# One fused kernel, one list of steps per slot: scaled keys, state and the low part of g ahead in the list, and the sums of squares one slot later

## The chip, the cores and the metric

The kernel runs on 1 core of one Trainium2 chip. A core has a matrix engine (PE, with its weight loads shown apart as PEld), a vector engine (DVE), an activation engine (ACT), a general engine (POOL) and a queue engine that issues DMAs (SP). Each runs its own list of instructions in order and waits at an instruction until what it needs is there. The metric is device time in microseconds (us) of one execution.

## The reference

Three stages follow each other: a gated linear attention, a feed-forward block with a cosine, and a gated feed-forward block on normalised rows.

```python
f = 1 / (1 + exp(-f_logit))                      # q, k, v, f_logit: (4, 8, 768, 48)
for t in range(768):
    state = f[t][:, None] * state + outer(k[t], v[t])
    y[t] = q[t] @ state                          # x = heads side by side: (3072, 384)
h = x @ w_in                                     # w_in (384, 2048)
x = (h * cos(h)) @ w_out                         # w_out (2048, 384)
rms = sqrt(mean(x * x, axis=-1) + 1e-6)
xn = x / rms * rms_g
g = xn @ w_gate                                  # w_gate, w_val (384, 1536)
out = (silu(g) * (xn @ w_val)) @ w_out2          # out (3072, 384)
```

## The kernel before

Every large product is made of three products of rounded parts: high times high, low times high and high times low. So each operand is split: ACT casts the high part, and POOL (or DVE) subtracts it to get the low part.

**Slots.** The first feed-forward block walks over 6 blocks of 512 rows and, in each, over 16 groups of 128 hidden columns. One group is a slot; slots 0 to 95 are these. Slots 96 to 167 are those of the second feed-forward block (6 blocks of 12). A slot n of the first kind does, by engine: 9 matmuls for h on PE (`m1_h`, L603, key `H`); on ACT the whole turns of the cosine's argument (`kint`, L612, `k`); on DVE the rest of the division (`wrap`, L618, `w`); on ACT the cosine (L624, `s`); on DVE g (L629, `g`); in the next slot the high part gh on ACT (L637, `hi`) and the low part gl on POOL (L644, `lo`); and two slots later 9 matmuls with `w_out` on PE (`m1_out`, L654). The h of a slot goes to one of two PSUM banks, so `H` of slot n+2 waits for g of slot n; gh and gl have two buffers each.

**Attention in between.** The attention runs in steps of 128 rows (24 steps; steps 0 to 4 are mostly done ahead, in a prologue). From slot 0 to slot 79 each slot takes one of the four pieces of a step on PE (key `P`, `piece_pe`): piece 0 turns the scaled keys (L348), piece 1 makes the scores (L357), piece 2 has nothing left to do in steps 9 and later, piece 3 makes the outputs and the next state's sum. Slot n has piece (n+1) mod 4. What the other engines do for a piece stands in the slot after it: ACT copies the turned keys out of PSUM (`kn`, L424), makes the gates (`tanh` in block 0: L267, L269; `grd` later: L255, L267); DVE runs two scans (`scan`: L281 makes E, L290) and scales k and q (`kt` L303, `qt` L312), adds the state (`st`, L455, L459); POOL copies each step's end of E (`pall`, L286, part of `scan`), spreads v (`vtl`, L292) and scales the state (`Tz`, L329, part of `cy`). All PSUM banks of the attention come from a ring of three, so a bank must be emptied before its third successor is taken.

**Weights.** In block 0 two weight tiles are decoded per slot, in the last block one (keys `t`, `x`, `f`): ACT L547, DVE L559 and L563, ACT L577, POOL L578.

**Sums of squares.** After a block, `m1_evac` (key `act`) empties three accumulators (L664 on DVE, L666 on ACT), POOL squares and adds (L674, L677; key `po`), and PE sums over partitions with a matmul of ones (`m1_sum`, L682, key `pe`), into the next bank of the ring. ACT copies the row (L684), and DMAs and POOL (L699, L700) make the reciprocal roots. `finish` sets in which slot each of these stands.

**The order.** Nothing schedules this: the strings of `SLOT` (block 0, blocks 1 to 4, block 5) and `SLOT2` (first block and the others of the second part) are the order in which a slot's keys are issued, and each engine gets its instructions in that order.

Of the kernel before, what the change touches and what calls it, by code (L numbers as in the profile page):

```python
# [27 lines left out]


SLOT = (  # L30
# [3 lines left out]
)  # L34
SLOT2 = (
    "gv pe t f dv x f sg t u act uh ul po x out ev",
    "gv pe ok act sg dv u uh ul po out ev",
)
PROLOGUE = (
# [10 lines left out]
def kernel(  # L50
# [15 lines left out]
    B, H, S, D = q.shape  # L66
# [52 lines left out]
    xh = [pp.tile([128, KD, 512], F32R, name=f"xh{i}") for i in range(2)]  # L119
    xl = [pp.tile([128, KD, 512], F32R, name=f"xl{i}") for i in range(2)]  # L120
# [8 lines left out]
    am = [ap_.tile([128, 512], F32, name=f"am{i}") for i in range(2)]  # L129
# [38 lines left out]
    st = {}  # L168
# [500 lines left out]
    def m1_store(j, x2):  # L669
        t0, N = blocks[j]  # L670
        nc.sync.dma_start(out=x2_d[:, t0:t0 + N].rearrange("(c p) t -> p c t", p=128), in_=x2)
# [15 lines left out]
    def m1_put(j, r):  # L687
        t0, N = blocks[j]
        nc.sync.dma_start(out=ss_d[t0:t0 + N].unsqueeze(0), in_=r)
# [7 lines left out]
    def m1_rinv(j, c):  # L697
        t0, N = blocks[j]
        nc.gpsimd.tensor_scalar(c, c, 1.0 / DM, EPS, op0=ALU.mult, op1=ALU.add)  # L699
        nc.gpsimd.tensor_tensor(out=c, in0=c, in1=mh.to_broadcast([128, N // 128]), op=ALU.pow)  # L700

    def m1_root(j, c):
        t0, N = blocks[j]
        nc.sync.dma_start(out=ri_d[t0:t0 + N].rearrange("(c p) -> p c", p=128), in_=c)
# [7 lines left out]
    gv = {}  # L712
# [122 lines left out]
    if True:  # L835
# [74 lines left out]
        pe_at, act_at, post_at, dve_at = {}, {}, {}, {}  # L910

        def at(table, slot, fn, *a):
            table.setdefault(slot, []).append((fn, a))
# [7 lines left out]
        held = {}  # L921
# [5 lines left out]
        def set_(key, fn, *a):  # L927
            held[key] = fn(*a)
# [5 lines left out]
        for n, (w, u) in enumerate(units):  # L934
            s = first + n * (4 * N2) // len(units)
# [3 lines left out]
        def finish(j, s, short):  # L939
            at(act_at, s + (1 if short else 2), lambda: set_((j, "x2"), m1_evac, j))  # L940
            at(post_at, s + 2, lambda: m1_store(j, held[j, "x2"]))
            for n, (fn, m) in enumerate(
                ((m1_sq, 0), (m1_sq, 1), (m1_add, 1), (m1_sq, 2), (m1_add, 2))
            ):
                at(post_at, s + 3 + n, lambda fn=fn, m=m: fn(held[j, "x2"], m))
            at(pe_at, s + 8, lambda: set_((j, "r"), m1_sum, j, held.pop((j, "x2"))))
            at(post_at, s + 9, lambda: m1_put(j, held.pop((j, "r"))))
            at(post_at, s + 10, lambda: set_((j, "c"), m1_get, j))
            at(post_at, s + 11, lambda: m1_rinv(j, held[j, "c"]))
            at(post_at, s + 12, lambda: m1_root(j, held.pop((j, "c"))))  # L950

        def norm(jj, s):
            at(post_at, s, m2_load, jj)
# [7 lines left out]
        for j, (t0, N) in enumerate(blocks):  # L961
# [21 lines left out]
            for i in range(N1):  # L983
# [42 lines left out]
                if len(outs) > 2:  # L1026
                    m1_out(*outs.pop(0))
                slot += 1
            finish(j, slot, final)
        m1_hi(*gp)  # L1030
        m1_lo(*gp)
# [283 lines left out]
```

## Time and profile before

| | |
|---|---|
| runs | 1029.33, 1031.47, 1030.81 us; median 1030.81 |
| profiled execution | 1034.35 us, span 1032.6 us |
| PE busy | 987.7 us (96%) |
| DVE busy | 631.2 us (61%) |
| ACT busy | 424.9 us (41%) |
| POOL busy | 327.8 us (32%) |

The profiled execution has 1.75 us around its span. The shares of busy time are means over stages that differ: up to about 568 us the first feed-forward block runs with the attention in between, and after that the second one alone. A busy PE includes matmuls that overlap, and matmuls at the lower of the two clock levels.

### The profile page before, as it was taken

To read this page: it belongs to the slowest core of one execution; us is meant where nothing else is said; L and a number is where in the kernel's file an instruction comes from. 1 tells how busy PE (TensorE), PEld (TensorE's weight loads), DVE (VectorE), ACT (ScalarE), POOL (GpSimd) and SP (SyncE) were. 2 spreads that over 40 slices of the span, in tenths; PEclk is the share of its full clock that TensorE was granted. 3 is DMA by queue.
4 is the path that set the end of the run, shared out by engine and by line. 5 is a ranking of instruction groups with operands and counts; after the bars stand their busy time and mean duration, and the time that the engine had idled before them with its cause. 6 is when DMAs were issued, how large, how long until landed. Compare 5 with 4: busy or idle time off the path is not lost.

```text
span 1032.6 us, 16330 instructions
## 1 busy us (share of the span) xinstructions
PE 987.7 (96%) x6286; PEld 819.1 (79%) x6286; DVE 631.2 (61%) x955; ACT 424.9 (41%) x747; POOL 327.8 (32%) x374
## 2 busy tenths in 40 slices
PE   7788999999899999989999999999999999999997
PEld 6666777778777777768877788888888888888886
DVE  6898976777777877775478666335335335335222
ACT  4466664445454454544667544212212212222111
POOL 2466654543533533363478354001001001001000
PEclk9899999999999999999999999999999999999999
DMA  8885323223222323311333453343343343332000
GB/s 163 195 198 135 85 52 81 51 53 100 65 64 51 86 61 72 95 23 17 108 117 92 138 169 87 92 133 92 108 133 94 114 139 92 123 117 62 31 1 34
DMA packets 123857, 96.14 MB, mean 93 GB/s; under 512 B 69238, under 2 KB 103030, under 8 KB 123772
## 3 DMA queue, kind: packets, MB, share of 16 engines
q1 hardware_dynamic: 123772, 95.03, 34.2%
q8 instruction: 51, 0.84, 0.3%
q14 instruction: 34, 0.28, 0.1%
HBM read 85.54 MB, written 9.46 MB: 92 GB/s over the span
## 4 chain that ended last, share of the span: by engine, by line
PE 67%; DVE 13%; ACT 7%; issue 4%; DMA 3%; POOL 3%; SPq 2%; DVEq 0%; ACTq 0%; POOLq 0%
PE bank L757 29%; PE bank L793 15%; PE bank L654 10%; PE bank L603 8%; DVE wrap L618 2%; DVE g L629 2%; ACT wrap L624 1%; DMA v_sb<-in_v_dram 1%; DVE E L281 1%; ACT gh L637 1%; ACT kint L612 1%; DVE ft L290 1%; POOL gl L644 1%; DVE qt L312 1%; PE bank L401 1%
## 5 line engine op out<-in xcount | busy, mean ns | idle before, releaser
L654 PE MATMUL bank<-gh,wo 128*128 128x512 f32 x576 | 208.3, 416 | 0.0
L771 DVE SCALAR_TENSOR_TENSOR u<-bank,sg 128x512 f32<-128x512 f32 x72 | 49.7, 691 | 201.3 <-PE bank L757 201.3
L644 POOL TENSOR_TENSOR gl<-g,gh 128x512 fp32r<-128x512 f32 x96 | 126.6, 1319 | 68.1 <-ACT gh L637 66.3
L654 PEld LDWEIGHTS bank<-gh,wo 128*128 128x128 f32 x576 | 111.2, 193 | 27.8 <-issue 1.6
L654 PE MATMUL bank<-gl,wo 128*128 128x512 f32 x288 | 117.9, 409 | 10.3 <-POOL gl L644 10.1
L757 PE MATMUL bank<-xh,wo 128*128 128x512 f32 x360 | 122.8, 395 | 0.0
L766 ACT ACTIVATE sg<-bank 128x512 f32<-128x512 f32 x72 | 43.1, 599 | 172.6 <-PE bank L757 172.6
L741 POOL TENSOR_TENSOR xl<-x2b,xh 128x512 fp32r<-128x512 f32 x18 | 24.2, 1344 | 283.1 <-ACT xh L740 283.1
L624 ACT ACTIVATE wrap<-wrap,cb 128x512 f32<-128x512 f32 x96 | 69.3, 722 | 101.1 <-DVE wrap L618 98.6
L778 ACT CAST uh<-u 128x512 fp32r<-128x512 f32 x72 | 44.7, 622 | 152.2 <-DVE u L771 152.0
L637 ACT CAST gh<-g 128x512 fp32r<-128x512 f32 x96 | 59.5, 620 | 100.3 <-DVE g L629 82.4
L629 DVE SCALAR_TENSOR_TENSOR g<-bank,wrap 128x512 f32<-128x512 f32 x96 | 66.0, 688 | 43.4 <-ACT wrap L624 40.5
L618 DVE SCALAR_TENSOR_TENSOR wrap<-bank,kint 128x512 f32<-128x512 f32 x96 | 65.8, 686 | 37.2 <-ACT kint L612 36.6
L784 DVE TENSOR_TENSOR ul<-u,uh 128x512 fp32r<-128x512 f32 x72 | 50.8, 705 | 48.9 <-ACT uh L778 48.9
L757 PEld LDWEIGHTS bank<-xh,wo 128*128 128x128 f32 x360 | 67.6, 188 | 14.6
L654 PEld LDWEIGHTS bank<-gl,wo 128*128 128x128 f32 x288 | 55.6, 193 | 28.5 <-POOL gl L644 16.4
L612 ACT ACTIVATE kint<-bank,cb 128x512 int32<-128x512 f32 x96 | 65.9, 686 | 27.7 <-PE bank L603 27.1
L793 PE MATMUL bank<-wo,uh 128*128 128x384 f32 x288 | 74.1, 338 | 0.0
L757 PE MATMUL bank<-xl,wo 128*128 128x512 f32 x180 | 71.0, 394 | 0.0
L793 PEld LDWEIGHTS bank<-wo,uh 128*128 128x128 f32 x288 | 52.7, 188 | 3.5 <-issue 0.5
L487 DVE SCALAR_TENSOR_TENSOR wacc<-stage,wacc 128x384 int32<-128x384 int32 x68 | 50.9, 748 | 0.7
L578 POOL TENSOR_TENSOR wo<-wx,wo 128x384 fp32r<-128x384 f32 x32 | 34.0, 1063 | 52.3 <-ACT wo L577 51.0
(343 smaller groups left out, 2222.3 us busy)
## 6 DMA issues: line engine op xcount, KB each, us to landing
stage<-in_moe_w_out_dram SPq DMA_DIRECT2D x56, 384.0 KB, 3.4
stage<-in_moe_w_gate_dram SPq DMA_DIRECT2D x24, 384.0 KB, 3.2
stage<-in_moe_w_val_dram SPq DMA_DIRECT2D x24, 384.0 KB, 3.2
stage<-in_moe_w_in_dram SPq DMA_DIRECT2D x16, 384.0 KB, 3.3
nat<-in_f_logit_dram SPq DMA_DIRECT2D x48, 96.0 KB, 3.0
nat<-in_k_dram SPq DMA_DIRECT2D x48, 96.0 KB, 2.3
nat<-in_q_dram SPq DMA_DIRECT2D x48, 96.0 KB, 2.2
v_sb<-in_v_dram SPq DMA_DIRECT2D x24, 192.0 KB, 2.7
```

Source lines behind the costliest of these rows:

```text
L487: nc.vector.scalar_tensor_tensor(out=wacc, in0=hi, scalar=1 << 30, in1=wacc, op0=ALU.bitwise_xor, op1=ALU.bitwise_and,)
L603: nc.tensor.matmul(t, l[:, 128 * kk:128 * (kk + 1)], r[:, kk, 0:N], start=idx == 0, stop=idx == 3 * KD - 1,)
L612: nc.scalar.activation(out=kt, in_=hb[j, i], func=AF.Identity, scale=INV2PI * UNIT, bias=cb[:, 0:1])
L618: nc.vector.scalar_tensor_tensor(out=w, in0=hb[j, i], scalar=INV2PI * UNIT, in1=kt, op0=ALU.mult, op1=ALU.subtract)
L624: nc.scalar.activation(out=w, in_=w, func=AF.Sin, scale=2.0 * math.pi, bias=cb[:, 1:2])
L629: nc.vector.scalar_tensor_tensor(out=g, in0=hb.pop((j, i)), scalar=UNIT, in1=w, op0=ALU.mult, op1=ALU.mult)
L637: nc.scalar.copy(out=h, in_=g)
L644: nc.gpsimd.tensor_tensor(out=l, in0=g, in1=h.bitcast(F32), op=ALU.subtract)
L654: nc.tensor.matmul(acc[m][:, 0:N], lw[:, cs], r, start=i == 0 and x == 0, stop=i == N1 - 1 and x == 2,)
L757: nc.tensor.matmul(t[y], l[:, 128 * kk:128 * (kk + 1)], r[:, kk, :], start=idx == 0, stop=idx == 3 * KD - 1,)
L784: nc.vector.tensor_tensor(out=l, in0=u, in1=h.bitcast(F32), op=ALU.subtract)
L793: nc.tensor.matmul(o2[tt][:, 0:DM], lu[:, cs], r, start=i == 0 and x == 0, stop=i == N2 - 1 and x == 2,)
```

## The change

Only the order changes. In block 0's list (`SLOT[0]`) the keys `st kn` come ahead of `tanh`, and `lo` comes right behind `hi`. In the list of blocks 1 to 4 `kn` comes first, and `lo` right behind `hi`. In the first list of the second part `act` comes first. `finish` puts the matmul of the sums, and the four steps behind it, one slot later.

```diff
 SLOT = (
-    "xh xl tanh hi H t kn x kt qt cy am st scan P k f w x grd f s t lo g po",
-    "tanh hi act H kn ff st kt xh xl qt cy am P k w grd scan s lo dv g pe po",
+    "xh xl st kn tanh hi lo H t x kt qt cy am scan P k f w x grd f s t g po",
+    "kn tanh hi lo act H st xh xl ff kt qt cy am P k w grd scan s dv g pe po",
     "act H hi k w lo P dv t pe s x g f po",
 )
 SLOT2 = (
-    "gv pe t f dv x f sg t u act uh ul po x out ev",
+    "act gv pe t f dv x f sg t u uh ul po x out ev",
     "gv pe ok act sg dv u uh ul po out ev",
 )
...
-            at(pe_at, s + 8, lambda: set_((j, "r"), m1_sum, j, held.pop((j, "x2"))))
-            at(post_at, s + 9, lambda: m1_put(j, held.pop((j, "r"))))
-            at(post_at, s + 10, lambda: set_((j, "c"), m1_get, j))
-            at(post_at, s + 11, lambda: m1_rinv(j, held[j, "c"]))
-            at(post_at, s + 12, lambda: m1_root(j, held.pop((j, "c"))))
+            at(pe_at, s + 9, lambda: set_((j, "r"), m1_sum, j, held.pop((j, "x2"))))
+            at(post_at, s + 10, lambda: m1_put(j, held.pop((j, "r"))))
+            at(post_at, s + 11, lambda: set_((j, "c"), m1_get, j))
+            at(post_at, s + 12, lambda: m1_rinv(j, held[j, "c"]))
+            at(post_at, s + 13, lambda: m1_root(j, held.pop((j, "c"))))
```

The first place is ACT in slot 12 (block 0), one of the slots with a piece 1. `kn` is the copy of the turned keys, the two `ft` rows are `tanh`, `gh` is the high part, and `wi15h` a weight's high part.

```order
 L624 ACTIVATE wrap<-wrap,cb 128x512
 L577 CAST wo<-wx 128x384
+L424 COPY kn<-bank_80 128x512
 L267 ACTIVATE ft_129<-bank_81 128x4x128
 L269 ACTIVATE ft_129<-ft_129,cb 128x4x128
 L637 CAST gh<-g 128x512
 L577 CAST wi15h<-wx 128x384
-L424 COPY kn<-bank_80 128x512
 L547 ACTIVATE wx<-stage,cb 128x384
 L612 ACTIVATE kint<-bank_77,cb 128x512
```

The copy moves ahead of four instructions, and `tanh` now stands behind it.

The second place is ACT from slot 24 to slot 26 (block 1): `kn` again, and `ssr`, the copy of the row of sums that the matmul of the sums made.

```order
 L624 ACTIVATE wrap<-wrap,cb 128x512
-L637 CAST gh<-g 128x512
 L424 COPY kn<-bank_80 128x512
+L637 CAST gh<-g 128x512
 L612 ACTIVATE kint<-bank_77,cb 128x512
 L255 ACTIVATE E,low<-ft_130,cb 128x4x128
 L267 ACTIVATE ft_130<-ft_130 128x4x128
 L624 ACTIVATE wrap<-wrap,cb 128x512
+L637 CAST gh<-g 128x512
+L612 ACTIVATE kint<-bank_78,cb 128x512
+L624 ACTIVATE wrap<-wrap,cb 128x512
 L684 COPY ssr<-bank_80 1x512
```

`kn` no longer waits behind the high part, and `ssr` stands one slot's work later, as its matmul does on PE.

The third place is POOL from slot 35 to slot 37 (block 2), first before, then now. `gl` is the low part, `Tz` the scaled state, `x2` the squares and their sums, `pall` the end of E.

```order
L329 TENSOR_TENSOR Tz_136<-Sn_2737,pall_87 48x4x32 x2
L329 TENSOR_TENSOR Tz_136<-Sn_2737,pall_87 48x4x16 x2
L644 TENSOR_TENSOR gl_2766<-g_2714,gh_2726 128x512
L674 TENSOR_TENSOR x2_2655<-x2_2655 128x512
L286 COPY pall_87<-E_2810 128x4
L644 TENSOR_TENSOR gl_2819<-g_2768,gh_2780 128x512
L674 TENSOR_TENSOR x2_2655<-x2_2655 128x512
```

```order
L644 TENSOR_TENSOR gl_2728<-g_2714,gh_2726 128x512
L329 TENSOR_TENSOR Tz_136<-Sn_2739,pall_87 48x4x32 x2
L329 TENSOR_TENSOR Tz_136<-Sn_2739,pall_87 48x4x16 x2
L674 TENSOR_TENSOR x2_2657<-x2_2657 128x512
L644 TENSOR_TENSOR gl_2784<-g_2768,gh_2782 128x512
L286 COPY pall_87<-E_2812 128x4
L674 TENSOR_TENSOR x2_2657<-x2_2657 128x512
```

Each low part moves ahead of the slot's other work on POOL: ahead of `Tz` in one slot, and ahead of `pall`, which waits for DVE's first scan, in the next.

## Rows read from the trace of the kernel before

**Rows 1.** Busy time in two stretches: start:end, length, PE, PEld, DVE, ACT, POOL, PEclk.

```profile
48.86:142.00 93.14, 81.39 (x588) 63.53 (x592) 85.05 (x130) 63.32 (x120) 61.03 (x60) 0.93 0.51 129
177.08:462.59 285.51, 273.59 (x2229) 216.44 (x2228) 223.21 (x326) 135.06 (x232) 122.79 (x149) 0.99 0.27 65
```

**Rows 2.** The same view, slots 24, 32, 40, 56, 72, 88; 33, 37; 97, 98.

```profile
192.19:202.00 9.81, 7.91 (x37) 5.79 (x36) 7.32 (x13) 4.82 (x9) 2.50 (x3) 0.83 0.41 95
237.25:242.70 5.45, 5.45 (x35) 4.27 (x34) 3.38 (x5) 4.08 (x8) 0.00 (x0) 1.00 0.59 141
279.78:287.68 7.90, 6.34 (x37) 4.65 (x36) 5.47 (x9) 4.83 (x9) 1.16 (x1) 1.00 0.48 115
366.95:374.03 7.08, 6.34 (x37) 4.65 (x36) 4.66 (x8) 4.83 (x9) 0.00 (x0) 1.00 0.54 130
453.08:462.59 9.51, 7.97 (x37) 5.55 (x36) 7.03 (x13) 4.82 (x9) 2.21 (x3) 0.82 0.01 2
530.45:537.79 7.34, 5.28 (x21) 3.68 (x20) 5.92 (x6) 4.26 (x9) 5.17 (x5) 1.00 0.19 54
242.70:246.89 4.19, 4.19 (x19) 3.30 (x18) 4.09 (x8) 1.67 (x3) 2.99 (x4) 1.00 0.00 0
262.64:268.85 6.21, 4.44 (x19) 3.30 (x18) 5.40 (x10) 3.21 (x7) 3.43 (x5) 1.00 0.23 59
576.19:584.25 8.06, 6.52 (x31) 5.35 (x30) 5.25 (x9) 3.62 (x7) 2.02 (x2) 1.00 0.35 104
584.25:590.54 6.29, 6.29 (x31) 5.48 (x31) 2.91 (x6) 2.10 (x5) 1.02 (x1) 1.00 0.68 226
```

**Rows 3.** PE's waits from 177 to 463 us: for whom, in total, times, longest.

```profile
PE bank L682 <- ACT kn L424: 5.7, 4, 1.9
PE bank L654 <- POOL gl L644: 5.1, 6, 1.8
```

**Rows 4.** The one wait of this kind in the whole trace.

```profile
PE bank L682 <- POOL x L677: 2.1, 1, 2.1
```

**Rows 5.** Timeline of slot 36 and its end: start, length, engine, [idle before <-releaser].

```profile
260.57 0.62 ACT L637 CAST gh<-g 128x512 fp32r<-128x512 f32 x1 [0.88 <-PE bank L357]
261.09 0.58 ACT L424 COPY kn<-bank 128x512 f32<-128x512 f32 x1
261.57 0.69 ACT L612 ACTIVATE kint<-bank,cb 128x512 int32<-128x512 f32 x1
...
262.30 0.69 DVE L618 SCALAR_TENSOR_TENSOR wrap<-bank,kint 128x512 f32<-128x512 f32 x1 [0.79 <-ACT kint L612]
...
265.69 0.68 DVE L629 SCALAR_TENSOR_TENSOR g<-bank,wrap 128x512 f32<-128x512 f32 x1
...
265.42 0.19 POOL L286 COPY pall<-E 128x4 f32<-128x4 f32 x1 [7.30 <-DVE E L281]
265.57 1.26 POOL L644 TENSOR_TENSOR gl<-g,gh 128x512 fp32r<-128x512 f32 x1
```

**Rows 6.** Timeline of slot 12 (block 0), the same columns.

```profile
126.09 0.72 ACT L269 ACTIVATE ft<-ft,cb 128x512 f32<-128x512 f32 x1
127.64 0.57 ACT L424 COPY kn<-bank 128x512 f32<-128x512 f32 x1
...
126.84 2.17 DVE L281 TENSOR_TENSOR_SCAN E<-ft,seed 128x516 f32<-128x516 f32 x1 [0.78 <-ACT ft L269]
...
128.27 1.16 PE L357 MATMUL bank<-qt,kt 48*128 48x128 f32 x14 [2.02 <-ACT kn L424]
```

**Rows 7.** DVE's two scans from 177 to 463 us: busy us, mean ns | idle.

```profile
L290 DVE TENSOR_TENSOR_SCAN ft<-ft,seed 128x516 f32<-128x516 f32 x13 | 19.6, 1505 | 0.0
L281 DVE TENSOR_TENSOR_SCAN E<-ft,seed 128x516 f32<-128x516 f32 x14 | 17.3, 1233 | 0.5
```

**Rows 8.** Timeline of slot 97, DVE and PE.

```profile
581.24 1.28 DVE L664 TENSOR_SCALAR x<-bank 128x512 f32<-128x512 f32 x2
...
582.07 0.58 PE L793 MATMUL bank<-xunit,uh 128*128 128x384 f32 x2 [1.54 <-ACT uh L778]
```

## The prediction

> **What bounds the kernel now.** I read the busy time by stretch first. In both stretches of [rows 1] PE looks nearly full, but who is full beside it differs. From 48.86 to 142 us (block 0, slots 0 to 14) DVE is busy for 85.05 of 93.14 us, PE for 81.39; DVE also holds the decode there. From 177.08 to 462.59 us (slots 21 to 72, most of blocks 1 to 4) PE is busy for 273.59 of 285.51 us, DVE for 223.21. After slot 97 PE runs without a gap: slot 98 is 6.29 us long with PE busy for 6.29 [rows 2].
>
> Then I read PE slot by slot, a slot beginning with its first matmul of `m1_h`. Slots of one kind should be equally long, and they are, but for a few. Slot 32, with scores, takes 5.45 us, and slot 33, without a piece, 4.19 us. Slots 24, 40, 56 and 72, with scores and the sum of squares, take 9.81, 7.90, 7.08 and 9.51, and slot 37, without a piece, 6.21 [rows 2]. The chain of PE's waits names two causes: the sum waits for `kn` 4 times, 5.7 us in all, and `m1_out` waits for gl 6 times, 5.1 us in all [rows 3].
>
> The timeline of slot 36 shows why [rows 5]. gh is done at 261.19, so gl could follow. But POOL stands at `pall` for 7.30 us until DVE's scan is done, and gl, behind it in the list, begins at 265.57, 4.4 us late. `kn` stands behind gh on ACT, and gh behind g on DVE, so whatever needs that bank (in slots 24, 40, 56, 72: the sum) waits for DVE.
>
> **The sums, one slot later.** PE is busy for 6.34 us in slots 40 and 56, against 5.45 in slot 32 [rows 2]: the sum itself costs 0.89 us. What the four slots have beyond a scores slot is 4.36 + 2.45 + 1.63 + 4.06 = 12.50 us. Less 4 x 0.89 that is 8.94 us. In slots 24 and 72 it is more than the wait, since the granted clock is 0.83 and 0.82 there: after the wait PE ran for a part of the slot at 1.2 GHz. One slot later `kn` is long done, there is no piece, and the squares on POOL have another slot; so the whole 8.94 goes, and 0.89 each is paid in slots 25, 41, 57, 73. Slot 88 waits for POOL's last add [rows 4]; 7.34 - 4.19 - 0.89 = 2.26 us go. **Together 11.2 us.** Above, no more is there to gain. Below, nothing, if the sum finds another wait in its new slot (a rival). The DMAs and POOL steps behind the sum (`m1_put`, `m1_get`, `m1_rinv`, `m1_root`) keep their distance to it. On SP the put stands as far behind its row as before, and the roots are read a block or more later.
>
> **gl right behind gh.** The 4.4 us are far more than any of the 6 waits, the longest of which is 1.8, so all **5.1 us** go. What comes behind gl on POOL now (`Tz`, `pall`, the squares) waits for gh, and is needed one to three slots later. Bounds: slot 37 alone is 2.02 us longer than slot 33 [rows 2] for a wait of at most 1.8, so a little more may come back; and nothing comes if DVE holds PE, which is the next question.
>
> **Can DVE follow?** 8.94 + 5.1 = 14.0 us on PE in slots 21 to 72 are real only if DVE's loop becomes shorter too, since `m1_h` of slot n+2 waits for g of slot n. g of slot 36 ends at 266.37 [rows 5] and slot 38 begins at 268.85 [rows 2]: PE can come 2.5 us closer. The gain in slot 72, 3.17 us, lies behind the last such meeting. What makes the loop itself shorter is `kn`: g, gh, kn, kint, wrap follow each other without a gap, and DVE is idle for 0.79 us before wrap [rows 5]. From the start of kn to that of kint it is 0.48 us; with kn ahead of gh, in the 0.88 us in which ACT waits for g anyway, this leaves the loop. 11 steps in this stretch copy turned keys: 5.3 us. A further 1.7 us are DVE's wait for PE after slot 24 (half of what the sums' two long slots cost in the mean, an estimate). Last, a low part that stands beside the second scan makes it longer. L290 and L281 scan the same 516 columns, but L290 takes 1.505 us in the mean and L281 1.233 [rows 7], and POOL has nothing to do beside L281, as it waits for it. gl comes earlier now; of 13 x 0.27 = 3.5 us I count half. So 2.5 + 3.2 + 5.3 + 1.7 + 1.8 = 14.5, just above 14.0. I take the whole 14.0; the lowest bound is 2.5 + 3.2 + 1.7 = 7.4, 6.6 less.
>
> **Block 0.** PE's waits there (2.02 us for `kn` in slot 12 [rows 6], and others for gl) go too, but I count them as **nothing**: DVE is the full engine, and PE, sooner at the next slot, waits there for a bank that DVE empties. If that cover were gone, PE's idle 93.14 - 81.39 = 11.75 us [rows 1] would be the prize. Against it stands a price. DVE's scan E waits 0.78 us for `tanh` [rows 6], and now `kn`, 0.57 us, comes ahead of `tanh`: in the slots with a `kn` (0, 8, 12) up to 3 x 0.57 = 1.7 us are added where DVE is full. Below, nothing, if DVE is held by POOL then anyway: E took 2.17 us beside POOL's work [rows 6], against 1.233. I take 1.1. The state ahead of the scaled keys on DVE changes no sum there.
>
> **Slot 97.** `act` first in the slot puts the evictions of block 5 ahead of the decode, of sg and of u. Now DVE does them at 581.24, and the first matmul into those banks follows at 582.07 [rows 8] (its wait is put down to uh, which is not the last). Slot 97 is 8.06 us long and slot 98 6.29 [rows 2]: **1.77 us** go. What is put behind them, the decode's steps, has DVE idle before u.
>
> **Sum.** 11.2 + 5.1 + 1.8 - 1.1 = 17.0 us. The profiled execution took 1034.35 us (1032.6 of span and 1.75 around it): 1017.3. The median of the runs, 1030.81, is 3.5 us below the profiled one, so I predict **1013.8 us** for a median. About 0.2% (2 us) is what a measurement of this kernel can tell from no change.
>
> **A rule on the two neighbours.** In block 0, where POOL works beside it, scan E took 2.17 us [rows 6]; alone, in blocks 1 to 4, it takes 1.233 [rows 7]. The Trainium skill (SBUF — State Buffer, Who interferes with whom) says that a vector instruction with two SBUF inputs and a GpSimd instruction that reads SBUF share a port, which one holds for its whole length while the other is blocked. By that rule the trace agrees, and it speaks against this change: gl, moved ahead, can hold up another scan.
>
> **The rivals.**
> *DVE's loop holds PE* (0.20). kn leaves the chain, but DVE is as late as before, since other waits (for ACT's cosine) fill in. For it speaks that DVE's loop leaves PE only 2.5 us of room; against it the gapless chain of [rows 5]. Then 6.6 us fewer: **1020.4**.
> *Block 0 is PE's after all* (0.08). Then 11.75 us come back there and the 1.1 isn't paid: **1001.0**. Against it: DVE's 85.05 of 93.14 us.
> *The sums only move their wait* (0.10): in slots 25, 41, 57, 73, 89 the bank or POOL's add is late again. Then 11.2 less: **1025.0**. Against it: `kn` is ahead of gh now, and POOL gets a slot more.
> *Slower: gl blocks the first scan* (0.05). Up to now POOL waits idle for E in blocks 1 to 4. If gl now lay beside E in each of 13 steps, E would take 2.17 instead of 1.233: 13 x 0.94 = 12.2 us on DVE's loop, and if L290 went from 1.505 to as much, 13 x 0.67 = 8.7 more. Loop: 20.9 - 5.3 = 15.6 longer; less 2.5 + 3.2 of room PE is 9.9 slower in these blocks, and with +1.1 and -2.26 - 1.77 elsewhere 7.0 us slower: **1037.8**. It decides from 13y = 5.3 + 5.7 + 2.9, so from y = 1.07 us per step. Against it: gh ends at 261.19, so gl of 1.26 us would be done by 262.5, while E ends at `pall`'s start, 265.42, and so begins at 264.2 [rows 5].
>
> **Range and chances.** The forecast has 0.57, from 1009 (more of L290, and slots that are shorter than the waits tell) to 1018 (kn in the loop half as much, and 1.7 in block 0). To leave no more than 0.2 out, the range takes in the rival of DVE's loop with some room and stops before the sums' and block 0's: **1005 to 1023**. Faster by over 0.2%: 0.92; slower: 0.05, the last rival; within 0.2%: 0.03, out of that of the sums.
>
> **What would show it.** Slots 24, 40, 56, 72 last 5.4 to 5.5 us, and 25, 41, 57, 73 some 5.1. No wait of `m1_out` for gl is left in blocks 1 to 4, and gl begins within 0.2 us of gh's end there. DVE's wait before wrap in slot 36 falls from 0.79 to about 0.3. Slot 97 lasts 6.3. Block 0 ends as late as before, or 1 to 2 us later. The prediction is wrong if PE's waits in blocks 1 to 4 return before `m1_h`, or if scan E grows beyond 1.3 us there.

## The result, and the profile after

The changed kernel takes 1018.62 us in the median of 6 runs (1015.7 to 1023.6), the kernel before 1031.14 us in 6 runs of the same session. The ratio is 0.9885, with a 95% interval from 0.9857 to 0.9913: 12 us faster, 9 to 15 by the interval. The profiled execution took 1019.26 us (span 1017.5), so it lies 0.6 us above its median, where that of the kernel before (1034.35) lay 3.2 us above.

First the busy time in stretches of the changed kernel: start:end, length, busy time of PE, PEld, DVE, ACT and POOL with the number of instructions, then PEclk, the granted clock of PE as a share of full speed, and two columns on DMA. The lines are slots 24, 25, 37, 46, 88, 89, 97, and block 0 from the first matmul of slot 0 to that of slot 15.

```profile
194.19:199.64 5.45, 5.45 (x35) 4.27 (x34) 3.39 (x5) 4.45 (x8) 2.16 (x2) 1.00 0.50 113
199.64:204.67 5.03, 5.03 (x21) 3.76 (x20) 4.84 (x10) 2.39 (x4) 2.65 (x3) 1.00 0.15 36
260.81:264.99 4.18, 4.18 (x20) 3.38 (x19) 4.07 (x8) 1.23 (x3) 2.43 (x4) 1.00 0.13 33
306.99:317.75 10.76, 7.83 (x107) 6.15 (x106) 5.64 (x8) 2.30 (x4) 2.04 (x2) 0.85 0.28 35
519.53:523.70 4.17, 4.17 (x19) 3.38 (x18) 3.27 (x5) 2.99 (x5) 3.09 (x4) 1.00 0.30 94
523.70:528.73 5.03, 5.03 (x21) 3.76 (x20) 3.86 (x6) 3.23 (x6) 2.69 (x3) 1.00 0.47 151
562.62:568.86 6.24, 6.24 (x31) 5.46 (x30) 3.81 (x8) 3.21 (x7) 1.01 (x1) 1.00 0.43 129
42.44:146.84 104.40, 87.05 (x617) 67.74 (x617) 92.50 (x139) 66.36 (x126) 66.81 (x69) 0.92 0.55 132
```

Against [rows 2], slot 24 fell from 9.81 to 5.45 and slot 37 from 6.21 to 4.18, slot 97 from 8.06 to 6.24, and the sum now costs 0.86 us in slots 25 and 89. Two lines went the other way. Block 0 is 104.40 us long, where the kernel before has 100.28 (44.56 to 144.84). And slot 46 is 10.76 us long, with 7.83 of PE and a clock of 0.85; before it took 7.54, and 6.34 in a second profile of the kernel before.

PE's waits of the changed kernel from 177 to 463 us, the answer to [rows 3], are down to one, which has no releaser ("issue") and lies in slot 46:

```profile
PE bank L654 <- issue: 2.9, 1, 2.9
```

The timeline of its slot 36 and the next one, ACT, DVE and POOL, beside [rows 5]:

```profile
257.64 0.62 ACT L637 CAST gh<-g 128x512 fp32r<-128x512 f32 x1 [0.41 <-PE bank L603]
...
258.33 1.29 POOL L644 TENSOR_TENSOR gl<-g,gh 128x512 fp32r<-128x512 f32 x1 [1.67 <-ACT gh L637]
...
258.88 0.69 DVE L618 SCALAR_TENSOR_TENSOR wrap<-bank,kint 128x512 f32<-128x512 f32 x1 [0.30 <-ACT kint L612]
...
262.01 0.19 POOL L286 COPY pall<-E 128x4 f32<-128x4 f32 x1 [2.38 <-DVE E L281]
```

gl follows gh at once and is done at 259.62, before POOL comes to `pall`. DVE waits 0.30 us before wrap, where it waited 0.79.

### The profile page after: what moved, and what is told of

It is laid out like the page before. It is cut to its first block, busy times and chain, and to the rows that moved or that the text cites. A ratio compares the mean times of both kernels' runs of the same rounds, so it can differ in the third digit from the quotient of the medians.

```text
span 1017.5 us, 16293 instructions
## 1 busy us (share of the span) xinstructions
PE 980.3 (96%) x6286; PEld 816.5 (80%) x6286; DVE 623.6 (61%) x955; ACT 424.3 (42%) x747; POOL 338.4 (33%) x374
## 4 chain that ended last, share of the span: by engine, by line
PE 82%; DVE 7%; DMA 3%; ACT 2%; SPq 2%; issue 2%; POOL 1%; DVEq 0%; ACTq 0%
PE bank L757 30%; PE bank L654 16%; PE bank L793 15%; PE bank L603 14%; PE bank L357 2%; DVE wx L559 2%; DMA raw_in<-in_moe_w_in_dram 2%; PE bank L401 2%; DVE wx L563 1%; DVE wrap L618 1%; SPq L187 1%; PE bank L415 1%; DVE g L629 1%; ACT wrap L624 1%; DMA v_sb<-in_v_dram 1%
## 5 line engine op out<-in xcount | busy, mean ns | idle before, releaser
L654 PE MATMUL bank<-gl,wo 128*128 128x512 f32 x288 | 115.5, 401 | 0.1
```

Source lines behind the costliest of these rows:

```text
L654: nc.tensor.matmul(acc[m][:, 0:N], lw[:, cs], r, start=i == 0 and x == 0, stop=i == N1 - 1 and x == 2,)
```

## Where DVE's time went

The prediction counted little on one thing that turned out large. These are DVE's groups in blocks 1 to 4 (177 to 463 us; busy us, mean ns | idle) that [rows 7] does not show, in the kernel before:

```profile
L303 DVE TENSOR_TENSOR kt<-kt,E 128x512 f32<-128x512 f32 x13 | 18.8, 1449 | 0.4
L312 DVE TENSOR_TENSOR qt<-qt,ft 128x512 f32<-128x512 f32 x13 | 12.5, 965 | 0.5
L323 DVE TENSOR_TENSOR Sn<-Sn,pall 128x192 f32<-128x192 f32 x11 | 8.9, 812 | 0.5
```

and in the changed kernel, with the scan L290 of [rows 7]:

```profile
L303 DVE TENSOR_TENSOR kt<-kt,E 128x512 f32<-128x512 f32 x14 | 21.6, 1544 | 0.5
L290 DVE TENSOR_TENSOR_SCAN ft<-ft,seed 128x516 f32<-128x516 f32 x14 | 17.3, 1239 | 0.0
L312 DVE TENSOR_TENSOR qt<-qt,ft 128x512 f32<-128x512 f32 x13 | 9.6, 738 | 0.5
L323 DVE TENSOR_TENSOR Sn<-Sn,pall 128x192 f32<-128x192 f32 x11 | 3.9, 350 | 0.5
```

The same operations on the same shapes became shorter: L290 by 0.266 us, L312 by 0.227, L323 by 0.462, while L303 grew by 0.095. Over 13, 13, 11 and 13 instructions that is 3.5 + 3.0 + 5.1 - 1.2 = 10.4 us less on DVE. Two stretches of the timeline show how. Before, in slot 37, gl has begun on POOL when the scan starts:

```profile
268.03 1.28 POOL L644 TENSOR_TENSOR gl<-g,gh 128x512 fp32r<-128x512 f32 x1
268.30 2.10 DVE L290 TENSOR_TENSOR_SCAN ft<-ft,seed 128x516 f32<-128x516 f32 x1
```

After the change, in the same slot, the scan begins first, and what POOL starts 0.09 us behind it is a copy:

```profile
264.89 1.23 DVE L290 TENSOR_TENSOR_SCAN ft<-ft,seed 128x516 f32<-128x516 f32 x1
264.98 1.23 POOL L292 COPY vtl<-v_sb 128x128 f32<-128x128 f32 x1
```

The scan takes 1.23 us instead of 2.10, and now the copy is the one that is long (0.28 us at 267.78 before). The other steps of these blocks look the same. Before, the 4 of 13 scans L290 that start 0.25 to 0.27 us behind a gl take 2.10 to 2.13 us, the other nine 1.22 to 1.25; after, all 14 take 1.23 to 1.25, and each copy that starts 0.08 to 0.10 us behind one takes 1.23 or 1.24. So whichever starts first goes through, and the other lasts until it is done. The Trainium skill (SBUF — State Buffer, Who interferes with whom) says just this, that the order of issue decides who blocks. By that rule the trace agrees. What the shorter operations are worth in time is a question of its own: gl also starts earlier now, and no run here has the one without the other.

## The experiments

Each set was timed against the kernel before on the same chip; a ratio is to that kernel, with its 95% interval behind it. An edit is shown against the changed kernel unless another one is named, and "..." stands where lines are left out.

**The change again, and three versions of it.** Two of these ask why DVE could follow PE.

> The change itself, once more, as the measure for the other three kernels of this set. Both theories expect about 1018.6 us and a ratio to before of 0.986 to 0.991. The wait of PE in slot 46 that has no releaser (3.3 us in the first profile) and the places of the half-rate stretches may differ; if slot 46 is long again, that wait belongs to the program and not to chance.

Measured: 1020.57 us, ratio 0.9902 (0.9877 to 0.9927); PE's wait in slot 46 is 4.3 us. So this wait belongs to the program.

```diff
-    "kn tanh hi lo act H st xh xl ff kt qt cy am P k w grd scan s dv g pe po",
+    "tanh hi lo kn act H st xh xl ff kt qt cy am P k w grd scan s dv g pe po",
```

> The change, but in blocks 1 to 4 kn stands behind the low part's two instructions again (behind gh on ACT). Theory of the prediction (kn's leaving is what shortens DVE's loop): the loop is 11 x 0.48 = 5.3 us longer between 177 and 463 us, DVE can no longer follow, and some 4.8 us are lost against the change: about 1023.5. Theory of the neighbours (DVE follows because POOL no longer works beside its instructions with two SBUF inputs: L290 1.505 to 1.239, L312 0.965 to 0.738, L323 0.812 to 0.350 in the mean): ACT's 15.6 us of waits for m1_h before kint take up the 5.3, PE waits for nothing, and the time is that of the change within 1 us.

Measured: 1020.60 us, 0.9902 (0.9878 to 0.9926), equal to the change (its repeat in the same set: 1020.57). L290 stays at 1.239 us, and DVE's idle time before wrap rises from 8.3 to 12.8 us between 177 and 463 us, without cost:

```profile
L618 DVE SCALAR_TENSOR_TENSOR wrap<-bank,kint 128x512 f32<-128x512 f32 x55 | 37.8, 687 | 12.8 <-ACT kint L612 12.1
```

This speaks against the prediction's main reason: `kn` leaves the loop, as it said, but DVE follows without that too.

```diff
-    "kn tanh hi lo act H st xh xl ff kt qt cy am P k w grd scan s dv g pe po",
+    "kn tanh hi act H st xh xl ff kt qt cy am P k w grd scan s lo dv g pe po",
```

> The change, but in blocks 1 to 4 the low part stands where it stood. Theory of the prediction: gl waits behind pall again, 5.1 to 7.3 us of PE's waits return, about 1024 to 1026. Theory of the neighbours: besides, L290, L312 and L323 are as long as before (1.5, 0.97, 0.81 us), which makes DVE's loop 10 us longer, and PE, which is 11.4 us earlier by the sums, waits for gl by what DVE is late: 8 to 11 us lost, about 1027 to 1030.

Measured: 1028.26 us, 0.9971 (0.9956 to 0.9986), 7.7 us slower than the change in the same session. Its profile has PE's waits for gl and the long scan and state again:

```profile
PE bank L654 <- POOL gl L644: 5.0, 7, 1.3
```

```profile
L290 DVE TENSOR_TENSOR_SCAN ft<-ft,seed 128x516 f32<-128x516 f32 x13 | 19.7, 1519 | 0.0
...
L323 DVE TENSOR_TENSOR Sn<-Sn,pall 128x192 f32<-128x192 f32 x11 | 8.9, 811 | 0.5
```

The waits alone are 5.0, the loss is 7.7: between the 5.1 to 7.3 of the prediction and the 8 to 11 of the neighbours, so the time does not decide between the two theories. That the scan and the state are long again is as the neighbours say.

```diff
-    "xh xl st kn tanh hi lo H t x kt qt cy am scan P k f w x grd f s t g po",
+    "xh xl tanh hi H t kn x kt qt cy am st scan P k f w x grd f s t lo g po",
```

> The change, but block 0 has its old list. Block 0 (from the first matmul of slot 0 to that of slot 15) took 104.4 us after the change and 100.3 before. Theory A (the order costs it: 1.5 us more of E's wait for tanh, the rest by gl beside the decode's instructions on DVE): 4.1 us return, block 0 takes 100 to 101 us, about 1014.5. Theory B (the difference is the granted clock, whose half-rate stretches lay elsewhere): block 0 stays at 103 to 104 us, and the time is that of the change within 1 us.

Measured: 1017.20 us, 0.9864 (0.9842 to 0.9887), 3.4 us faster than the change in the same session; block 0 takes 101.83 us. So the order costs block 0 some 2.6 us in the profile and 3.4 in the medians. The old list of block 0 gives 100.28, 100.27, 100.82, 101.83 and 101.90 us in five profiles, the new one 104.40, 104.45, 104.62 and 103.84 in four, so the order costs block 0 time, as theory A says, with a price of 3.3 us by the two means (101.0 and 104.3), less than its 4.1.

**One part alone, and block 0 apart.**

> The kernel before, once more, for the 3.5 us by which its profiled execution (1034.35) lay above the median (1030.81). Theory A (that offset is chance: half-rate stretches fell into slots 24 and 72, which cost them 1.9 and 1.6 us more than slot 40's 7.90): in another profile some of these slots last 7.1 to 8.0 us, and the profiled execution is nearer to the median, 1030 to 1032. Theory B (the wait of the sum brings the half rate each time): slots 24 and 72 last 9.5 to 9.8 us again, and the offset stays unexplained.

Measured: 1029.96 us, ratio 1.0 (0.9986 to 1.0013), profiled 1029.0. Slots 24 and 72 of this profile:

```profile
189.06:197.34 8.28, 6.36 (x37) 4.65 (x36) 5.86 (x9) 4.83 (x9) 1.55 (x1) 1.00 0.44 102
...
447.37:456.83 9.46, 7.92 (x37) 5.66 (x36) 6.96 (x13) 4.82 (x9) 2.16 (x3) 0.82 0.01 2
```

Slot 24 came at the full clock this time, though it is longer than the 7.1 to 8.0 us of theory A; slot 72 was at the lower clock for a part of its length again, as theory B says. The larger difference lies before slot 0, first in the profile that I predicted from, then in this one:

```profile
0.00:44.56 44.56, 35.09 (x452) 29.33 (x452) 33.34 (x76) 17.80 (x34) 12.80 (x37) 0.92 0.82 174
```

```profile
0.00:41.46 41.46, 33.13 (x452) 27.76 (x453) 33.35 (x76) 17.82 (x34) 12.97 (x37) 1.00 0.82 175
```

That is 3.1 us; slot 24 adds 1.5, and slot 46 1.2 by a wait at the full clock. In the set above, the 17 executions of the kernel before run from 1027.83 us at a mean granted clock of 0.993 to 1034.48 at 0.985, and the profile that I predicted from had 0.986. By and large the longer executions are those with the lower mean clock. Of the stretches at the lower clock named here, slot 72's is in both profiles, those before slot 0 and in slot 24 are in one.

The sum and the four steps behind it one slot later, as in the change, and nothing else (against the kernel before):

```diff
-            at(pe_at, s + 8, lambda: set_((j, "r"), m1_sum, j, held.pop((j, "x2"))))
+            at(pe_at, s + 9, lambda: set_((j, "r"), m1_sum, j, held.pop((j, "x2"))))
...
```

> The kernel before with the sum of squares and what follows it one slot later, and nothing else. Theory of DVE's loop (in blocks 1 to 4 PE gains only what DVE can follow, and gl, which waits behind pall for DVE, eats the rest): 3.2 in slot 72, 2.3 in slot 88 and 1.7 at slot 24, some 7.5 us, about 1024.0; PE's waits for gl grow from 5.1 to 8 to 10 us. Theory of independent terms: the whole 11.2 to 11.4 us, about 1020.1, and the waits for gl stay at 5.1.

Measured: 1030.57 us, ratio 1.0 (0.9986 to 1.0013): nothing in all, less than either theory gave. Slots 24 and 25 show why:

```profile
190.15:195.60 5.45, 5.45 (x35) 4.27 (x34) 3.98 (x6) 2.21 (x4) 1.51 (x1) 1.00 0.46 105
195.60:202.40 6.80, 5.29 (x22) 3.68 (x20) 5.73 (x10) 3.79 (x8) 2.94 (x4) 1.00 0.22 53
```

Slot 24 is as short as in the changed kernel, and PE waits in the next one instead. Between 177 and 463 us its waits for gl are up from 5.1 us to what the first line says, and the second is slot 46 again:

```profile
PE bank L654 <- POOL gl L644: 9.4, 10, 1.8
PE bank L654 <- issue: 2.7, 1, 2.7
```

The slots with the sum, before and now, still are 4.6 us shorter together than in the kernel before of this set, mostly slots 72 and 88. That is used up by the longer slots 46 (10.03 us, 6.34 before) and 47, 4.7 us together, and slot 94 (5.58, 4.19). So the zero has two causes: PE's waits for gl one slot later, and the wait in slot 46, which goes with the later write of the roots (see below).

```diff
-    "xh xl st kn tanh hi lo H t x kt qt cy am scan P k f w x grd f s t g po",
+    "xh xl tanh st kn hi lo H t x kt qt cy am scan P k f w x grd f s t g po",
```

> The change, but in block 0 tanh stands ahead of st and kn. Theory A (two prices in block 0, E's wait for tanh 1.5 us and gl beside the decode 2.6): block 0 takes 102.5 to 103 us, E waits 0.6 us in each of its four steps, 1.5 us faster than the change, about 1018. Theory B (gl ahead of the decode is the whole price): block 0 stays at 104 to 104.5, about 1019.5.

Measured: 1019.10 us, 0.9894 (0.9874 to 0.9914); block 0 takes 102.83 us, and DVE's idle time before E falls from 3.9 to 2.4 us over the four steps. So block 0 of this profile is 1.6 us shorter, as theory A says; the ratio is no better than the change's (0.9885 and 0.9902).

```diff
-    "xh xl st kn tanh hi lo H t x kt qt cy am scan P k f w x grd f s t g po",
+    "xh xl st kn tanh hi H t x kt qt cy am scan P k f w x grd f s t lo g po",
```

> The change, but in block 0 the low part stands at its old place, late in the slot. Theory A (two prices): block 0 takes 101.5 to 102 us, L559's mean on staged weights falls from 0.993 back to about 0.80 us, 2.6 us faster than the change, about 1017. Theory B (gl ahead of the decode is the whole price): block 0 takes 100.3 to 101, 3.5 to 4 us faster, about 1015.5.

Measured: 1017.36 us, 0.9877 (0.9855 to 0.9898); block 0 takes 100.63 us. So gl's price is 3.8 us in block 0 of the profile, larger than estimated: by block 0 this is theory B's number, by the median theory A's. With `tanh0` both prices show in block 0. DVE's decode of the staged weights and the scan L290 carry the price of gl. In block 0 of the changed kernel:

```profile
L559 DVE SCALAR_TENSOR_TENSOR wx<-stage,wx 128x384 int32<-128x384 int32 x16 | 15.9, 993 | 3.2 <-ACT wx L547 3.2
...
L290 DVE TENSOR_TENSOR_SCAN ft<-ft,seed 128x516 f32<-128x516 f32 x4 | 8.0, 1995 | 0.0
```

and with the low part late in the slot again:

```profile
L559 DVE SCALAR_TENSOR_TENSOR wx<-stage,wx 128x384 int32<-128x384 int32 x16 | 12.7, 795 | 3.2 <-ACT wx L547 3.2
...
L290 DVE TENSOR_TENSOR_SCAN ft<-ft,seed 128x516 f32<-128x516 f32 x4 | 6.5, 1620 | 0.0
```

**The low part alone, and versions that go further.** The first edit is against the kernel before, the second against the change, the third against the second.

```diff
-    "tanh hi act H kn ff st kt xh xl qt cy am P k w grd scan s lo dv g pe po",
+    "tanh hi lo act H kn ff st kt xh xl qt cy am P k w grd scan s dv g pe po",
```

> The kernel before with the low part right behind the high part in blocks 1 to 4, and nothing else; the counterpart to the sums alone, which gave nothing. Theory of the neighbours (the low part's place frees DVE: L290 1.24, L312 0.74, L323 0.35 us in the mean, 10 us less on DVE in slots 21 to 72): PE's waits for gl (5.1 us) go, the sums' waits get shorter too, since kn follows DVE's loop: 6 to 8 us, about 1023. Theory that the two parts are worth something only together: DVE is early, but the sums still hold PE by as much as before, and 2 us or less are gained, about 1028.

Measured: 1019.32 us, 0.9890 (0.9869 to 0.9911). That is 9.8 us, more than the 6 to 8 of the neighbours' theory: one key moved in one string gives about as much as the whole change. The rest of the change is not nothing, though. By slots of the two profiles the change gains 6.5 us over this version (the sums 4.3, slot 97 1.8, slots 93 and 94 0.4), and loses 5.9 again (slots 46 and 47 3.4, block 0 2.5). L290 takes 1.258 us in the mean, L312 0.736, L323 0.351; PE waits for gl nowhere in blocks 1 to 4, and less than before for kn:

```profile
PE bank L682 <- ACT kn L424: 1.9, 3, 0.9
```

```diff
-    "xh xl st kn tanh hi lo H t x kt qt cy am scan P k f w x grd f s t g po",
+    "xh xl tanh st kn hi H t x kt qt cy am scan P k f w x grd f s t lo g po",
...
-            at(post_at, s + 12, lambda: m1_rinv(j, held[j, "c"]))
-            at(post_at, s + 13, lambda: m1_root(j, held.pop((j, "c"))))
+            at(post_at, s + 14, lambda: m1_rinv(j, held[j, "c"]))
+            at(post_at, s + 15, lambda: m1_root(j, held.pop((j, "c"))))
```

> The change with block 0 as before but for st and kn, which come behind tanh, and with the reciprocal root and its write two slots later (s + 14 and s + 15). Block 0: if the two prices add, it takes 99 to 100 us (104.4 after the change, 100.6 with the low part alone put back); if the tanh price is only seen when gl is early, 100.3 to 100.8. Slot 94: the root's two POOL instructions no longer stand between gl and the normalisation's low part, so it takes 4.2 us instead of 4.6 to 5.6. Slot 46: if PE's unnamed wait there has to do with the write of the roots just ahead, it falls from 2.9 to 4.4 us to at most 1; if not, it stays. In all about 1014 with that wait and 1010.5 without.

Measured: 1014.01 us, 0.9844 (0.9818 to 0.9869). Block 0 takes 99.92 us, so its two prices, 1.6 and 3.8 us one by one, are 4.5 together. Slot 94 takes 4.17, and slot 46 takes 6.35 without a wait. But slot 82 took 8.49 us, which is my edit's doing: SP waits for POOL at the write of block 3's roots,

```profile
SPq L704 <- POOL ssc L700: 23.2, 1, 23.2
```

and the first loads of the next decode stand behind it and are issued at 471.86 us.

```diff
-            at(post_at, s + 14, lambda: m1_rinv(j, held[j, "c"]))
-            at(post_at, s + 15, lambda: m1_root(j, held.pop((j, "c"))))
+            at(post_at, s + (12 if j == 3 else 14), lambda: m1_rinv(j, held[j, "c"]))
+            at(post_at, s + (13 if j == 3 else 15), lambda: m1_root(j, held.pop((j, "c"))))
```

> The last version, but the reciprocal root of block 3 and its write stay in their old slots, 76 and 77. If the wait in slot 82 (8.49 us, PE for ACT, which had waited 3.3 us for the staged weights) came from the write of that root, behind which the first three loads of the next decode stand on SP (it waited 23.2 us for POOL, and they were issued one to two slots later), slot 82 lasts 4.2 us and 4.3 us are gained: about 1010. If the loads were late for another reason, slot 82 stays long: 1014. Slot 46 stays at 6.3 to 7.5 us if the roots' place is what matters there, and goes back to 9.5 to 12 if its short wait was chance.

Measured: 1010.14 us, 0.981 (0.9783 to 0.9837): the fastest version, 19.1 us faster than the kernel before. The forecast of 1010 for a write of the roots that holds back the loads came true. The loads are issued at 462.57 us and slot 82 takes 4.17 us. From 146 to 1000 us no wait of PE is left.

The fastest version with the sum back at s + 8, m1_put at s + 9 and m1_get at s + 10:

```diff
-            at(pe_at, s + 9, lambda: set_((j, "r"), m1_sum, j, held.pop((j, "x2"))))
+            at(pe_at, s + 8, lambda: set_((j, "r"), m1_sum, j, held.pop((j, "x2"))))
...
```

> The same version with the sum of squares back in its old slot (s + 8, and the two steps behind it). What the sum's move is worth once DVE's loop is short: by the slots of the low part alone (7.29, 6.76, 6.88 and 7.32 us in slots 40, 56, 72, 88, against 5.45 or 4.17, less 0.86 for the sum itself) 4.3 us, so about 1014.3. By the prediction's term 11.2 us, so about 1021. If the sum's waits are the same as before the change (5.7 us for kn and 2.1 for POOL), 7.8.

Measured: 1012.80 us, 0.9836 (0.9808 to 0.9863), 2.7 us more than that version, less than each of the three guesses. In slots 24 and 88 (the sum back in its old place) PE has the work of the scores and the sum without a gap, and waits for POOL:

```profile
188.69:194.99 6.30, 6.30 (x37) 4.66 (x36) 4.31 (x7) 4.88 (x9) 2.43 (x3) 1.00 0.55 129
...
509.35:516.66 7.31, 5.28 (x21) 3.69 (x20) 5.89 (x6) 4.24 (x9) 5.15 (x5) 1.00 0.19 54
```

Slots 40, 56 and 72 last 6.30 too. So with gl and kn early the sum waits for kn nowhere, and its later slot is worth slot 88's wait of 2.0 us and little else.

**The wait in slot 46.** The load of q in that slot is issued in four DMAs by SP, the queue engine. Its third issue in the second profile of the kernel before, in the changed kernel and in the fastest version is as follows (start, length):

```profile
311.58 2.54 SPq L210 DMA_DIRECT2D nat<-in_q_dram  x1
```

```profile
310.37 2.83 SPq L210 DMA_DIRECT2D nat<-in_q_dram  x1
```

```profile
305.21 1.00 SPq L210 DMA_DIRECT2D nat<-in_q_dram  x1
```

Where the roots are written one slot ahead of that load (eight kernels: the change, its repeat and six versions), PE waits 2.7 to 4.4 us in slots 46 and 47 with no releaser. Where they are written two slots ahead (three profiles), it waits 0 or 0.9 us; where one slot behind (three), not at all. That the place of the write goes with the wait is shown; why PE stops for it is not. The long issue is not enough: the kernel before has one too (2.85 and 2.54 us in its two profiles), and PE waits 0.9 and 0 us there. In all eleven profiles with the write ahead, by one slot or two, a 16 KB packet of instructions (DMA queue 8) starts within 0.7 us of the first issue of that load and takes 2.6 to 3.4 us, where about 1.0 is the median of its queue. In the three with the write behind it takes 0.9 to 1.0. Whether PE waits for that packet is not shown.

## Why the prediction was right, and where it was not

The range held the time and the direction was right. The centre, 1013.8, was 4.8 us too fast, and part of the sum stood on the wrong legs. That it came no further off owes something to luck: by the profile, gl was worth 2.2 us more than its term, while block 0 cost 3.0 more than its own and slots 46 and 47 took 3.4 that the prediction had not counted.

- **Sums, one slot later (11.2).** As slot lengths it holds: slots 24, 25, 40, 41, 56, 57, 72 and 73 together are 9.1 us shorter (8.94 forecast), 88 and 89 2.3 (2.26 forecast). As a term that stands by itself it does not. Alone, the move gains nothing: PE's waits come back one slot later, for gl (9.4 us where it was 5.1), and slots 46 and 47 take the rest. Undoing it in the fastest version costs 2.7. The rival of DVE's loop, that PE can gain only what DVE lets it, fits this term better; the rival of the sums named the right slots, but the wait there is for gl, and not for the bank or POOL's add. And 1.5 us of slot 24 were a half-rate stretch that the second profile does not have.
- **gl behind gh (5.1).** No wait is left, and slots 29, 37, 45, 49, 53, 61, 65 and 69 are 7.3 us shorter. It is worth more: alone about 10 us in the medians of its set (1029.13 to 1019.32), and the sum's waits for `kn` shrink with it (5.7 to 1.9 us).
- **Can DVE follow?** The answer was right, the reasons were mis-sized. "A low part that stands beside the second scan makes it longer" was counted as 1.8 us for L290 alone; it is 3.5 us shorter instead, and with L312 and L323, which I did not look at, and L303, which grew, 10.4 shorter. Of the 5.3 us of `kn` 4.5 appear as DVE's idle time when it is put back, but they are not needed. What `kn` does is to free the sum: at its old place the sum waits for `kn` 1.9 us with the low part alone, and nowhere in the fastest version with the sum put back. How much of the gain is DVE's shorter work and how much gl's earlier start is argued, not shown.
- **Block 0 (1.1).** This is the step that failed most. E's wait for `tanh` rose by 1.5 us, as bounded; but nothing was counted for gl itself, which now stands beside the decode and the scan L290 there: 3.8 us in the profile. The rule that I cited from the Trainium skill (SBUF — State Buffer, Who interferes with whom) speaks of any vector instruction with two SBUF inputs. The trace agrees: the decode L559 went from 0.795 to 0.993 us in the mean and L290 from 1.620 to 1.995. I had applied it to the scan E alone, which in fact became shorter (2.084 to 1.295). The stretch of [rows 1] that stands for block 0 leaves out the first 4.3 us of slot 0 and the last 2.8 us of slot 14, which changes nothing in the argument.
- **Slot 97 (1.77).** 1.81 by slot lengths.
- **Not seen at all:** slots 46 and 47, 3.4 us, and slots 93 to 95, where 0.4 were gained.
- **From one execution to the median.** I carried the 3.5 us between profile and median over as if both kernels had them. Mostly they were half-rate stretches of that one execution (3.1 us before slot 0 and 1.5 in slot 24 against the second profile), so the profiled gain (1034.35 to 1019.26, 15.1 us) is more than the medians' 12.5.

By its own profile: 9.1 + 2.3 + 7.3 + 1.8 + 0.4 less 3.4 and 4.1 gives 13.4; another 2.1 come from before slot 0, which begins at 42.44 us instead of 44.56. That is 15.5, and slot 99 does begin 15.4 us earlier. But the 2.1 are the half-rate stretch, and so chance: the second profiles of both kernels (1029.0 and 1020.42 us) have slot 0 at 41.46 and 41.68, lose 6.6 us in slots 46 and 47, and are only 8.6 us apart. The medians' 12.5 lies between the two.

## What to carry to other kernels

Terms that hang on one loop are not added: take each part away from the whole, and also try it alone, since here the largest term of the sum was worth 0 alone and 2.7 in the whole, and a smaller one 10 alone. Look also for what a part costs elsewhere: the move of the sums lost 4.7 us in two slots where nothing had been meant to change. Before an instruction of POOL is moved, list which of DVE's instructions with two SBUF inputs it leaves and which it comes to stand beside, in every stage that the same table sets. And a step that is moved back in a DMA queue takes along the loads that stand behind it.

## What the runs showed of the hardware

- A small state update on DVE (L323, 128x192) takes 0.350 us in the mean after the change and 0.812 before, where POOL's squares lay beside 6 of 11 (1.07 to 1.32 us each, the others 0.35); a copy on POOL (L292) takes 0.28 us alone and 1.23 behind a scan that began 0.09 us earlier.
- The scaled keys from PSUM (kt from a bank and E) took 0.68 us in block 0 with POOL at work beside all of them; from SBUF (kt and E, L303) 1.449 and 1.544 us in the mean.
- A DMA issue of the same load (its third) took 0.42 to 3.35 us at the same place of the program. PE stopped there for 2.7 to 4.4 us without a releaser when a small write had gone ahead a slot earlier, and for at most 0.9 us when it had gone two slots ahead or came behind. What links them is open.
